# Loading the row of shift_k first and spreading it over the partitions during the warm-up

## The chip, the core and the metric

The kernel runs on one core of a Trainium2 chip. The core has TensorE (PE: matrix products; PEld: its weight loads), VectorE (DVE), ScalarE (ACT), GpSimd (POOL) and SyncE (SP), each with a queue of its own that it works through in order, and 16 DMA engines that all queues share. The metric is the time of one execution on the device, in microseconds (us); shown are the median of several runs and one execution recorded by the profiler.

## The reference

The reference is a forward pass of two branches and all of its gradients. S is 2048, D is 512, F is 1376, all tensors are bf16.

```python
xn = layernorm(q)                                  # no weights
k_shift = sum over t of k_pad[:, t:t+S] * shift_k[:, 3-t]     # four taps
kv = k_shift * v
y = causal_conv(kv, ssm_k) + kv * ssm_D            # by FFT over 2S
h = (xn @ w_gate) * (xn @ w_up)
out = q + xn * y + h @ w_down
# and the gradients of out with grad_out: q, k, v, shift_k, ssm_k, ssm_D, w_gate, w_up, w_down
```

shift_k has the shape (512, 4): four taps for each of the 512 channels. In the kernel the rows of the sequence lie over the 128 partitions and the channels along the free dimension, so each partition needs all 2048 numbers of shift_k. The tile skb (128 x 4 x 512) holds them, the same in each partition.

## The kernel before

The 2048 positions are held as 128 partitions times 16 rows, and worked on in eight chunks of two rows. A main strand (main, with ffn1 and yb inside) does the gated products of a chunk: up and gate into pgu (L512), the gradient through w_down into pdh (L518), products of them on VectorE (L532, L533), then output and input gradient (py, px). A side strand (side, with front and then groups) does the convolution: front forms k_shift and kv and takes all signals through the first half of the transform; groups does the spectral part. A pacing rule takes steps of the two strands in turn. Then follow the weight gradients and the rest.

Two kinds of order meet. From L656 to first.close() in tables(3), the order of the instructions on TensorE, VectorE and ScalarE is the order in which the program states them (a manual schedule). After that, the tile framework's planner orders each engine's instructions by its own estimate of when each is ready and by priorities (high_priority with SOON). So an instruction taken out can change the order of others.

**The front of the program, L643 to L669.** The transfers are issued first. load_x(0) loads the first two rows of q and grad_out on SyncE's queue (x_b, go_b); load_w on ScalarE's queue loads the first part of the weights w_down, w_up and w_gate (Wd, Wu, Wg); SyncE's queue goes on with the other weight parts, the second chunk, the row skr of shift_k (L650, one partition, 2048 numbers, 4 KB), the row of ssm_D, ssm_k (ssk, 2 MB) and further rows. A transfer has to wait for an earlier one, most often the eighth before it, because eight semaphores are used in turn. Then TensorE does 36 warm-up products of the identity with itself (warm, L658: transposes whose result nobody reads), VectorE forms small tables and the statistics of the first chunk (norm_stats, L664), TensorE transposes go_b (pe_t, L665) and the first part of Wd (wd_transposes, L666); ScalarE takes the square root (norm_std, L333) and copies both transposes out of PSUM (gt, WdT; the helper act, L235); VectorE normalizes the rows (norm_rows, L339 and L342) and copies their transpose (xt, L238). Another ten warm-up products follow (L669), then the products of ffn1 for chunk 0: pdh first, then pgu. ScalarE's Sin for the tables (L76) and its square root need different function tables, which an ACT_TABLE_LOAD instruction brings in.

**The spread of shift_k, L704 to L712.** It is the second half of late_loads, which front calls for b = 0, behind the four table steps. load_k issues the transfers of k (tile kh, L311 to L315). Then skr is spread: for each half of the 512 channels, two products of a column of ones (one partition, 128 wide; "rows" in the profile) with 128 channels x 4 taps of skr, 512 columns each, into a PSUM tile pskb of the pool P2 (three buffers). A copy brings each half from PSUM to skb and turns the order from channel-tap to tap-channel: half 0 on ScalarE (act, L235), half 1 on VectorE (dve, L238). skb is first read by pre(0) at L391, for ks_b, and in the backward pass at L1104.

Around it in the side strand: kernel_spec transposes ssk on TensorE (ptk, L415), VectorE copies that to SBUF (kn, L238), stage1 multiplies (pf, L370) and the result is copied to fst by ScalarE or, one of four, VectorE. norm(2), norm(3) and so on take statistics of the next rows (L326, L327).

Of the kernel before, what the change touches and what calls it, by code (L numbers as in the profile page):

```python
# [8 lines left out]
BF = mybir.dt.bfloat16  # L9
# [9 lines left out]
D = 512  # L19
F = 1376  # L20
R = 16
P = 128
# [168 lines left out]
def kernel(  # L191
# [24 lines left out]
    nc = tc.nc  # L216
# [17 lines left out]
    def act(o, i):  # L234
        nc.scalar.copy(o, i)  # L235
# [16 lines left out]
    def P2(name, shape, dt=F32):  # L252
        return ps2.tile(shape, dt, name=name, tag="p2")

    def P1(name, shape, dt=F32):
        return ps1.tile(shape, dt, name=name, tag="p1")

    ident = const.tile([P, P], BF, name="ident")
# [3 lines left out]
    skb = const.tile([P, 4, D], BF, name="skb")  # L262
# [11 lines left out]
    ones = rows[:, 1, 0:128]  # L274
# [6 lines left out]
    stp = st_es.enter_context(tc.tile_pool(name="stp", bufs=2, side="right"))  # L281
# [13 lines left out]
    def load_x(b):  # L295
        load_go(b, load_q(b))

    def load_q(b):
        x = stp.tile([P, 2, D], BF, name="x_b", bufs=4)
        nc.sync.dma_start(x[:], x_n[:, 2 * b:2 * b + 2, :])  # L300
        return x

    def load_go(b, x):
        go = stp.tile([P, 2, D], BF, name="go_b", bufs=3)
        nc.sync.dma_start(go[:], go_n[:, 2 * b:2 * b + 2, :])
        XG[b] = (x, go)

    def load_k():
        for i, t in enumerate(hds):
            z = t[96:97, NFB - 1].rearrange("p t s -> p (t s)")  # L310
            nc.sync.dma_start(ST["kh"][0:1, 0:3, :].rearrange("p r d -> p (r d)")[:, 768 * i:768 * i + 768], z)  # L311
        nc.sync.dma_start(ST["kh"][1:113, 0:3, :], k_n[0:112, R - 3:R, :])
        nc.sync.dma_start(ST["kh"][113:128, 0:3, :], k_n[112:127, R - 3:R, :])
        for r0 in range(0, R, R // 2):
            nc.sync.dma_start(ST["kh"][:, 3 + r0:3 + r0 + R // 2, :], k_n[:, r0:r0 + R // 2, :])  # L315

    def norm(b):
        norm_stats(b)
        norm_rows(b)
# [15 lines left out]
    def norm_rows(b):  # L335
        x, go = XG[b]
        rb = slice(2 * b, 2 * b + 2)
        xn = x
        nc.vector.reciprocal(rstd[:, rb], rstd[:, rb])  # L339
        for i in range(2):  # L340
            r = 2 * b + i
            nc.vector.tensor_scalar(xn[:, i, :], x[:, i, :], mv[:, r, 0:1], rstd[:, r:r + 1],  # L342
                                    op0=ALU.subtract, op1=ALU.mult)
        XG[b] = (xn, go)
        if b > 1:
            store_xn(b)
        NORMED.add(b)
# [4 lines left out]
    def load_v(b):  # L352
        v = stp.tile([P, 2, D], BF, name="v_b")
        nc.sync.dma_start(v[:], v_n[:, 2 * b:2 * b + 2, :])
        VB[b] = v
# [53 lines left out]
    def kernel_spec():  # L409
        def tr(r0):  # L410
            pt = P2("ptk", [P, 4, D], BF)
            for i in range(4):
                for c in range(NC4):
                    src = ssk[:, c, :].rearrange("d (p r) -> d r p", r=R)[:, r0 + i, :]
                    nc.tensor.transpose(pt[:, i, cs(c)], src, ident[:])  # L415
            kn = ST["st1"].tile([P, 4, D], BF, name="kn", tag="kn", bufs=KNB)
            with tc.high_priority(offset=SOON):
                dve(kn[:], pt[:])
            return kn
        kn = tr(0)  # L420
        yield
        for r0 in range(0, R, 4):
            for i in range(4):
                stage1(0, kn, i, r0 + i, dve if i == 2 else act)
                if i == 1 and r0 + 4 < R:
                    nx = tr(r0 + 4)
                yield
            kn = nx

    def wd_transposes(fa, fe):  # L430
        c0, c1 = 128 * fa, min(F, 128 * fe)
        m = 4 if fe - fa <= 4 else 2
        for ca in range(0, NC4, m):
            pw = P2("pw", [P, m, 16 // m * 128], BF)
            for c in range(ca, ca + m):
                for fb in range(fa, fe):
                    f0, fw = FBLK[fb]
                    nc.tensor.transpose(pw[:, c - ca, (fb - fa) * 128:(fb - fa) * 128 + fw], Wd[:fw, fb, cs(c)], ident[:fw, :fw])
            (act if ca or not fa else dve)(WdT[:, ca:ca + m, c0:c1], pw[:, :, :c1 - c0])
# [26 lines left out]
    def pe_t(src, name, eng):  # L466

        pt = P1("px8", [P, 2 * NC4, P], BF)
        for i in range(2):
            for c in range(NC4):  # L470
                nc.tensor.transpose(pt[:, NC4 * i + c, :], src[:, i, cs(c)], ident[:])
        t = xtp.tile([P, 2, NC4, P], BF, name=name)
        to = t[:].rearrange("p r c s -> p (r c) s")
        eng(to, pt[:])
        return t

    def warm(src, n):

        pt = P1("warm", [P, P], BF)
        for _ in range(n):  # L480
            nc.tensor.transpose(pt[:], src[:], ident[:])
# [15 lines left out]
    def ffn1(ch):  # L497
# [3 lines left out]
        for fb0 in range(0, NFB, 2):  # L501
# [21 lines left out]
            if ch == 0 and fb0 == 0:  # L523
                wd_transposes(*WPARTS[1])
            gu = gup.tile([P, 2, 2, 256], BF, name="gu")
# [3 lines left out]
            if ch == 0 and fb0 == 4:  # L529
                wd_transposes(*WPARTS[2])  # L530
            with tc.high_priority(offset=SOON):
# [101 lines left out]
    def load_w(eng, fa, fe):  # L633
        c0, c1 = 128 * fa, min(F, 128 * fe)
        full = (c1 - c0) // 128
        eng.dma_start(Wd[:, fa:fa + full, :], B_w_down[c0:c0 + 128 * full, :].rearrange("(fb p) d -> p fb d", p=128))
        if c0 + 128 * full < c1:
            eng.dma_start(Wd[:c1 - c0 - 128 * full, fa + full, :], B_w_down[c0 + 128 * full:c1, :])
        for W, src in ((Wu, B_w_up), (Wg, B_w_gate)):
            eng.dma_start(W[:, :, c0:c1], src[:, c0:c1].rearrange("(c p) f -> p c f", p=128))  # L640

    WPARTS = ((0, 2), (2, 6), (6, NFB))
    load_x(0)  # L643
    load_w(nc.scalar, *WPARTS[0])
    load_w(nc.sync, *WPARTS[1])
    x1 = load_q(1)
    load_w(nc.sync, *WPARTS[2])
    load_go(1, x1)
    skr = stp.tile([1, D, 4], BF, name="skr", tag="fst", bufs=4)
    nc.sync.dma_start(skr[:], A_shift_k.rearrange("(o d) j -> o d j", o=1))  # L650
    nc.sync.dma_start(Drow, A_ssm_D.rearrange("(o d) -> o d", o=1))
    nc.sync.dma_start(ssk[:], A_ssm_k.rearrange("(c p) s -> p c s", p=128))
    load_v(0)
# [1 line left out]
    load_v(1)  # L655
    first = ExitStack()  # L656
    first.enter_context(tc.manual_schedule(engines={nc.vector.engine, nc.scalar.engine, nc.tensor.engine}))
    warm(ident, 36)  # L658
    TB.forward_base()
    TB.inverse_base()  # L660
    TB.inverse_phases()
# [3 lines left out]
    gt0 = pe_t(XG[0][1], "gt", act)  # L665
    wd_transposes(*WPARTS[0])  # L666
    norm_rows(0)
# [33 lines left out]
            first.close()  # L701
            open_st1()

    def late_loads():  # L704
        load_k()

        for h in range(2):
            pb = P2("pskb", [P, 2, D])
            for q in range(2):
                d0 = 256 * h + 128 * q  # L710
                nc.tensor.matmul(pb[:, q, :], lhsT=ones, rhs=skr[:, d0:d0 + 128, :].rearrange("o d j -> o (d j)"), start=True, stop=True)
            (act, dve)[h](skb[:, :, 256 * h:256 * h + 256], pb[:].rearrange("p q (d j) -> p j (q d)", j=4))  # L712

    def front():
        for b in range(8):
            if b == 0:
                late_loads()
                with tc.issue_after(TB.last.ins):
                    norm(2)
            elif b < 6:  # L720
                norm(b + 2)
            if LATE:
                LATE.pop(0)()
            yield
            if b == 0:
                yield from kernel_spec()
                yield from wgu_transposes()
                WTS.append(True)
            if 0 < b < 7:
                load_v(b + 1)  # L730
            yield from pre(b)
            if b < 5:
                load_x(b + 3)
        LATE.pop(0)()
        yield
# [38 lines left out]
    pace = [170 / 71]  # L774
    gpool["es"] = ExitStack()
    side = seq(front(), groups())


# [448 lines left out]
```

## Time and profile before

| | |
|---|---|
| median of three runs | 480.31 us (479.93 to 480.77) |
| the profiled execution | 480.12 us |
| its span, first to last instruction | 478.3 us |
| busy in the span: PE, PEld | 469.2 us, 312.7 us |
| busy: DVE, ACT, POOL | 340.3 us, 305.6 us, 13.9 us |
| moved by DMA | 139.85 MB, mean 292 GB/s |
| first real product (pdh, L518) | starts at 9.17 us |
| the four products of pskb | from 25.75 us |
| first use of skb (ks_b, L391) | 36.30 us |

Times inside the profile count from the span's start. In a timeline row stand the start, the length (of the whole group, where several alike are merged), engine, line, operation, what is written and read, the count, and in brackets how long the engine was idle before it and what released it. In the page's slices a digit is the busy share of one fortieth of the span in tenths; 9 means 90% or more. A product counts as busy from its issue to its modelled end, so products in a row overlap.

### The profile page before, as it was taken

To read this page: it belongs to the slowest core of one execution; us is meant where nothing else is said; L and a number is where in the kernel's file an instruction comes from. 1 tells how busy PE (TensorE), PEld (TensorE's weight loads), DVE (VectorE), ACT (ScalarE), POOL (GpSimd) and SP (SyncE) were. 2 spreads that over 40 slices of the span, in tenths; PEclk is the share of its full clock that TensorE was granted. 3 is DMA by queue.
4 is the path that set the end of the run, shared out by engine and by line. 5 is a ranking of instruction groups with operands and counts; after the bars stand their busy time and mean duration, and the time that the engine had idled before them with its cause. 6 is when DMAs were issued, how large, how long until landed. Compare 5 with 4: busy or idle time off the path is not lost.

```text
span 478.3 us, 10403 instructions
## 1 busy us (share of the span) xinstructions
PE 469.2 (98%) x4293; PEld 312.7 (65%) x4293; DVE 340.3 (71%) x609; ACT 305.6 (64%) x349; POOL 13.9 (3%) x30
## 2 busy tenths in 40 slices
PE   8999999999999999999999999999999999999997
PEld 7876755547648547447447743566777787777785
DVE  6789989989366567686767877122257799599991
ACT  4957777759567778779779976275676545233241
POOL 8000000000000000000000000110000000000000
PEclk9999999999999999999999999999999999999999
DMA  8999899898998968967977469999999989999937
GB/s 273 375 378 365 295 299 312 314 322 313 313 295 291 265 199 267 279 205 246 293 240 240 153 236 357 348 330 318 328 383 379 372 264 321 319 270 281 286 134 238
DMA packets 111100, 139.85 MB, mean 292 GB/s; under 512 B 38827, under 2 KB 84304, under 8 KB 109518
## 3 DMA queue, kind: packets, MB, share of 16 engines
q1 hardware_dynamic: 109470, 137.85, 89.2%
q10 hardware_dynamic: 1584, 1.36, 1.0%
q8 instruction: 33, 0.54, 0.5%
q14 instruction: 13, 0.11, 0.1%
HBM read 67.08 MB, written 63.41 MB: 273 GB/s over the span
## 4 chain that ended last, share of the span: by engine, by line
PE 75%; DMA 12%; DVE 9%; SPq 1%; issue 1%; ACT 1%; ACTq 0%; DVEq 0%
PE px L555 14%; PE pgu L512 13%; PE pu L1050 11%; PE py L548 7%; PE pd L1014 6%; PE pdh L518 6%; PE pt L847 4%; PE pq L920 3%; PE ps L584 3%; PE pf L370 3%; PE pg L613 3%; DMA ssk<-in_A_ssm_k_dram 3%; DMA natT<-HDD 2%; DMA hb<-HDD 2%; DMA x_b<-in_A_q_dram 2%; DMA XN<-x_b 1%
## 5 line engine op out<-in xcount | busy, mean ns | idle before, releaser
L555 PE MATMUL px<-WT,hd 128*128 128x512 bf16 (+1 forms) x352 | 81.0, 380 | 0.0
L1050 PEld LDWEIGHTS <-xnC 128*128 128x128 bf16 x704 | 67.1, 98 | 8.3 <-issue 0.6
L555 PEld LDWEIGHTS <-hd 128*128 128x128 bf16 (+1 forms) x352 | 32.8, 98 | 44.4 <-issue 7.7
L235 ACT CAST gu<-pgu 128x1024 bf16<-128x1024 f32 (+1 forms) x48 | 45.4, 946 | 16.6 <-PE pgu L512 16.3
L235 ACT CAST GO<-pg 128x1024 bf16<-128x1024 f32 x48 | 46.3, 1016 | 13.7 <-issue 7.2
L235 ACT CAST SP<-ps 128x1024 bf16<-128x1024 f32 x47 | 45.6, 1027 | 13.7 <-PE ps L584 11.8
L600 DVE TENSOR_TENSOR T<-SP 128x2048 bf16<-128x2048 bf16 x24 | 29.4, 1223 | 34.8 <-ACT SP L235 34.7
L512 PE MATMUL pgu<-xt,Wu 128*128 128x256 bf16 (+1 forms) x352 | 53.1, 273 | 0.7 <-DVE kn L238 0.6
L512 PE MATMUL pgu<-xt,Wg 128*128 128x256 bf16 (+1 forms) x352 | 52.8, 273 | 0.0
L1050 PE MATMUL pu<-natd,xnC 128*128 128x256 bf16 x448 | 51.2, 273 | 0.0
L518 PE MATMUL pdh<-gt,WdT 128*128 128x256 bf16 (+1 forms) x352 | 46.9, 273 | 0.2 <-ACT WdT L235 0.2
L235 ACT CAST fst<-pf 128x1024 bf16<-128x1024 f32 x44 | 42.8, 1032 | 5.5 <-ACT fst L235 2.0
L512 PEld LDWEIGHTS <-Wu 128*128 128x128 bf16 (+1 forms) x352 | 33.0, 100 | 15.1 <-issue 10.2
L548 PE MATMUL py<-Wd,hd 128*128 128x512 bf16 (+1 forms) x176 | 41.4, 380 | 0.0
L235 ACT CAST og<-pu 128x1024 bf16<-128x1024 f32 (+1 forms) x11 | 10.9, 993 | 42.6 <-PE pu L1050 30.3
L518 PEld LDWEIGHTS <-WdT 128*128 128x128 bf16 (+1 forms) x352 | 34.9, 100 | 5.0 <-ACT WdT L235 0.4
L512 PEld LDWEIGHTS <-Wg 128*128 128x128 bf16 (+1 forms) x352 | 34.9, 100 | 3.6
L235 ACT COPY natd<-pt 128x2048 bf16<-128x2048 bf16 x14 | 26.2, 1875 | 12.2 <-PE pt L847 12.2
L533 DVE TENSOR_TENSOR hd<-gu,dh 128x1024 bf16<-128x1024 bf16 (+1 forms) x48 | 30.8, 642 | 0.8
L532 DVE TENSOR_TENSOR hd<-gu 128x512 bf16<-128x512 bf16 (+1 forms) x48 | 19.1, 398 | 16.0 <-ACT gu L235 16.0
L548 PEld LDWEIGHTS <-hd 128*128 128x128 bf16 (+1 forms) x176 | 16.5, 98 | 20.8 <-issue 3.1
L600 DVE TENSOR_TENSOR U<-SP 128x2048 bf16<-128x2048 bf16 x24 | 29.2, 1218 | 0.0
(177 smaller groups left out, 692.9 us busy)
## 6 DMA issues: line engine op xcount, KB each, us to landing
HDD<-hd SPq DMA_DIRECT2D x35, 384.0 KB, 4.6
FD<-fst SPq DMA_DIRECT2D x24, 512.0 KB, 4.9
X<-FD SPq DMA_DIRECT2D x24, 512.0 KB, 5.6
GD<-GO SPq DMA_DIRECT2D x24, 512.0 KB, 3.8
g<-GD SPq DMA_DIRECT2D x11, 1024.0 KB, 8.9
hb<-HDD SPq DMA_DIRECT2D x7, 1344.0 KB, 11.0
bb<-BX SPq DMA_DIRECT2D x8, 512.0 KB, 4.8
BX<-bx SPq DMA_DIRECT2D x7, 512.0 KB, 4.0
```

The lines of the kernel that those rows point to most:

```text
L235: nc.scalar.copy(o, i)
L370: nc.tensor.matmul(pf[:, c, :], lhsT=TB.W1[:, c, :], rhs=src[:, i, :], start=True, stop=not point)
L512: nc.tensor.matmul(pgu[:w, i, t, :], lhsT=W[:, c, f0:f0 + w], rhs=xt[:, :, c, :], start=(c == 0), stop=(c == NC4 - 1))
L518: nc.tensor.matmul(pdh[:w, i, :], lhsT=WdT[:, c, f0:f0 + w], rhs=gt[:, :, c, :], start=(c == 0), stop=(c == NC4 - 1))
L532: nc.vector.tensor_tensor(hd[:fw, fb0:fb0 + n, 0, :], gu[:fw, :n, 0, :], gu[:fw, :n, 1, :], op=ALU.mult)
L533: nc.vector.tensor_tensor(hd[:fw, fb0:fb0 + n, 1:3, :], gu[:fw, :n], dh[:fw, :n].unsqueeze(2).to_broadcast((fw, n, 2, 256)), op=ALU.mult)
L548: nc.tensor.matmul(py[:], lhsT=hd[:fw, fb, 0, ss], rhs=Wd[:fw, fb, :], start=(fb == 0), stop=(fb == NFB - 1))
L555: nc.tensor.matmul(px[:], lhsT=hd[:fw, fb, t, ss], rhs=W[:fw, fb, :], start=(t == 1 and fb == 0), stop=(t == 2 and fb == NFB - 1))
L600: tt(W[:].rearrange("p c a d -> p c (a d)"), A[:, i:i + 1].rearrange("p c a d -> p c (a d)").to_broadcast((P, 2, 2 * D)), B[:].rearrange(" ...
L847: nc.tensor.transpose(pt[:, r, :fw], hs[:, (r % 2) * 128:(r % 2) * 128 + 128], ident[:fw, :fw])
L1014: nc.tensor.matmul(pd[:fw, :], lhsT=nat_h(fb, r), rhs=goC[:, r, :], start=(r == 0), stop=(r == R - 1))
L1050: nc.tensor.matmul(pu[:, c, :, :fw], lhsT=xnC[:, r, cs(c)], rhs=nat_d(fb, r), start=(r == 0), stop=(r == R - 1))
```

## The change

The transfer of skr goes from its place on SyncE's queue to the head of ScalarE's queue, ahead of the first weights. The spread (the new function spread_k) is stated inside the warm-up: 14 warm-up products, the four products of the spread, ten more, 24 in place of 36. Both copies to skb are on ScalarE. Since all this lies in the manually scheduled front, the four products and the two copies stand where they are written: ahead of the transposes of go_b on TensorE, ahead of the square root on ScalarE. late_loads goes; front calls load_k alone.

```diff
+    def spread_k():
+        for h in range(2):
+            pb = P2("pskb", [P, 2, D])
+            for q in range(2):
+                d0 = 256 * h + 128 * q
+                nc.tensor.matmul(pb[:, q, :], lhsT=ones, rhs=skr[:, d0:d0 + 128, :].rearrange("o d j -> o (d j)"), start=True, stop=True)
+            act(skb[:, :, 256 * h:256 * h + 256], pb[:].rearrange("p q (d j) -> p j (q d)", j=4))
+
     WPARTS = ((0, 2), (2, 6), (6, NFB))
+    skr = stp.tile([1, D, 4], BF, name="skr", tag="fst", bufs=4)
+    nc.scalar.dma_start(skr[:], A_shift_k.rearrange("(o d) j -> o d j", o=1))
     load_x(0)
     load_w(nc.scalar, *WPARTS[0])
...
     load_go(1, x1)
-    skr = stp.tile([1, D, 4], BF, name="skr", tag="fst", bufs=4)
-    nc.sync.dma_start(skr[:], A_shift_k.rearrange("(o d) j -> o d j", o=1))
     nc.sync.dma_start(Drow, A_ssm_D.rearrange("(o d) -> o d", o=1))
...
-    warm(ident, 36)
+    warm(ident, 14)
+    spread_k()
+    warm(ident, 10)
...
-    def late_loads():
-        load_k()
-
-        for h in range(2):
-            pb = P2("pskb", [P, 2, D])
-            for q in range(2):
-                d0 = 256 * h + 128 * q
-                nc.tensor.matmul(pb[:, q, :], lhsT=ones, rhs=skr[:, d0:d0 + 128, :].rearrange("o d j -> o (d j)"), start=True, stop=True)
-            (act, dve)[h](skb[:, :, 256 * h:256 * h + 256], pb[:].rearrange("p q (d j) -> p j (q d)", j=4))
-
     def front():
         for b in range(8):
             if b == 0:
-                late_loads()
+                load_k()
```

## The prediction

> **What bounds the kernel now.** I read the page first: who is busy, and when.
>
> ```profile
> PE 469.2 (98%) x4293; PEld 312.7 (65%) x4293; DVE 340.3 (71%) x609; ACT 305.6 (64%) x349; POOL 13.9 (3%) x30
> ...
> PE   8999999999999999999999999999999999999997
> ...
> DVE  6789989989366567686767877122257799599991
> ACT  4957777759567778779779976275676545233241
> ```
>
> The span of 478.3 us is TensorE's: it is busy for 469.2 of it. So the sum is short: the end moves with the work that TensorE has once it runs, and with its idle time. That idle time, 9.1 us, lies mostly in the first 60 us. Second view, the timeline of the first 13 us:
>
> ```profile
> 4.80 0.69 DVE L326 BATCH_NORM_STATS2 stats<-x_b 128x6 f32<-128x512 bf16 x1 [0.81 <-DMA x_b<-in_A_q_dram]
> ...
> 6.11 1.03 PE L471 MATMUL px<-ident,go_b 128*128 128x128 bf16 x8 [0.65 <-DMA go_b<-in_grad_out_dram]
> ...
> 6.54 0.30 ACT L333 ACTIVATE rstd<-mv,eps_t 128x2 f32<-128x2 f32 x1 [2.97 <-DVE mv L327]
> ...
> 7.18 1.01 ACT L235 COPY gt<-px 128x1024 bf16<-128x1024 bf16 x1 [0.35 <-PE px L471]
> ...
> 8.09 1.02 ACT L235 COPY WdT<-pw 128x1024 bf16<-128x1024 bf16 x1
> ...
> 9.13 1.28 ACT L76 ACT_TABLE_LOAD   x1
> ```
>
> ScalarE's queue opens the gate: square root, copy of gt, copy of WdT, and the first real product (pdh, L518) starts at 9.17, right after that last copy. Nothing later makes up for a delay there: the table of stretches shows TensorE busy 4.00 of 4 us from 12 to 20, and none of its waits from 9.17 to 25 us is for a transfer. Third view, the timeline where the row of shift_k is spread today and what follows:
>
> ```profile
> 25.75 1.03 PE L711 MATMUL pskb<-skr,rows 1*128 1x512 bf16 x4
> ...
> 26.42 1.03 ACT L235 CAST skb<-pskb 128x1024 bf16<-128x1024 f32 x1
> ...
> 26.71 1.22 PE L415 MATMUL ptk<-ident,ssk 128*128 128x128 bf16 x16
> ...
> 27.79 1.22 DVE L238 CAST skb<-pskb 128x1024 bf16<-128x1024 f32 x1
> ...
> 28.93 1.22 DVE L238 COPY kn<-ptk 128x2048 bf16<-128x2048 bf16 x1
> ...
> 30.20 0.38 PE L370 MATMUL pf<-kn,W 128*128 128x512 bf16 x1 [0.20 <-DVE kn L238]
> ...
> 36.30 0.69 DVE L391 TENSOR_TENSOR ks_b<-kh,skb 128x1024 bf16<-128x1024 bf16 x1 [1.51 <-DMA kh<-in_A_k_dram]
> ...
> 44.37 0.59 PE L370 MATMUL pf<-kn,W 128*128 128x512 bf16 x2 [0.51 <-DVE kn L238]
> ```
>
> Here VectorE is the pacemaker. It is busy without a gap from 40 to 52 and nearly so to 60, and TensorE waits for it. Fourth view, stretches of 4 us (length, then busy time and count on PE, PEld, DVE, ACT, POOL, then clock, DMA share, GB/s):
>
> ```profile
> 40.00:44.00 4.00, 3.86 (x38) 3.04 (x36) 4.00 (x9) 2.25 (x4) 0.00 (x0) 1.00 1.02 379
> 44.00:48.00 4.00, 3.09 (x23) 2.23 (x23) 4.00 (x8) 2.89 (x5) 0.00 (x0) 1.00 1.07 299
> 48.00:52.00 4.00, 3.66 (x35) 2.71 (x33) 4.00 (x8) 3.26 (x4) 0.00 (x0) 1.00 1.06 298
> 52.00:56.00 4.00, 3.65 (x29) 2.83 (x29) 3.93 (x7) 1.83 (x4) 0.00 (x0) 1.00 1.03 379
> ```
>
> Over the eight stretches from 28 to 60 TensorE is idle for 2.0 of 32 us; the waits name kn and fst copies of VectorE for about 1.8 of that. From 64 to 128 it is busy 4.00 in nearly every stretch, so a lead or a lag at 60 us reaches the end.
>
> **The change, part by part.**
>
> *Taken out at 25.7 us.* Four products of 512 columns: the next work (ptk) starts at 26.71 instead of 25.74, so at most 0.97; by their spacing, (1.03 - 0.37)/3 = 0.22 each, 0.88. I take **-0.9**. ScalarE's copy (1.03) goes too, where ScalarE has room (busy 1.29 of the next 4 us): nothing. VectorE's copy (1.22) goes from the engine that sets the pace: below.
>
> *Put in at the front, TensorE.* 14 products in place of 36, at (4.02 - 0.31)/35 = 0.106 apart, end at 1.44 + 14 x 0.106 = 2.9. Then TensorE waits for skr, and its queue with it: ten warm-up products and the transposes of go_b. When does skr land? The trace has no transfer of one row at the start. Lower bound: the last ACT issue of the kernel, alone on the queues, is at 475.49, its first packet at 476.35, its last landing signal at 476.69; 1.2 us after 0.72 and some 0.45 to the waiting engine (x_b's last signal at 4.36, VectorE starts at 4.80) give 2.4, which means no wait. Upper bound: x_b, issued at the same moment, at 4.80. Between: the ACT queue's first packet today comes only at 2.66, 1.94 after its issue; plus 0.17 (first packet to last signal, as at 476) and 0.45 gives **3.3**. I take it, because it is the row of that very queue and moment. The clock is not open yet: the records show 313 ns for a 128-column warm-up product against 219 after the clock opens at 7.41. So a 512-column product needs 4 x 0.106 = 0.42: half one is in PSUM at 3.3 + 0.85 + 0.2 = 4.35, half two at 5.2. Ten products more end at 6.1, as go_b lands (6.11). TensorE itself is not late; the 12 warm-up products dropped stood in that wait.
>
> *Put in at the front, ScalarE.* The skr issue (0.35, as SP's for it at 11.54) goes ahead of three issues that end at 2.26: they end at 2.6. Wd, Wu and Wg of the first part start 0.35 later; the last lands near 9.3 and is used at 10.49, so that is covered. The order of the changed program, as built, has **two table loads** where there was one: one ahead of the skb copies, another ahead of the square root. First load to 3.95; copies, 1.03 each as at 26.42, from 4.4 to 6.46; second load, 1.28, to 7.75; square root at 7.75 instead of 6.54, 1.21 late. Its statistics are ready at 6.5, so nothing hides this except the 0.35 that ScalarE waits at 7.18 today. gt and WdT end 0.86 later, and pdh starts at 10.0: **+0.86**. VectorE's normalized rows come 1.2 late, xt at 10.3; the products that read it follow eight pdh (0.87) and start at 10.9: hidden. Bounds from the two landings: 2.9 or earlier gives +0.46 (then the matmuls and copies alone count), 4.8 gives 2.70 - 0.35 = +2.35.
>
> The Trainium skill (ScalarE: Activation LUTs, "What ACT_TABLE_LOAD costs") says that a switch of set takes 1283 ns plus some 1380 ns of drain. The load at 9.13 here starts 0.02 us after the copy before it ends, and the next activation starts at 10.42, 1.29 after the load's start: no drain shows. With that drain the front would cost 0.86 + 1.38 = 2.24 by the page, and the sum would be near rival 4's.
>
> *The queues.* skr leaves SP; each later transfer moves up one place, and most wait for the transfer eight places earlier. The DMA engines are saturated from 4 us on (share 1.0 to 1.1), so bytes and not issues decide. ssk, 2 MB, still lands near 25.1 and still holds back the stores and loads behind it; kh still lands near 36.3. Bounds: the wait of 0.5 us that one SP issue has there, either way.
>
> *The planner's new order.* VectorE loses 1.22 of copying ahead of kh and starts its front work about 0.9 late. As built, it now does one more bn_stats (0.67) and the two rows of norm 2 (0.73) ahead of the first ks_b. It ends ks_b near 37.0, against 37.64 today for ks_b and those rows, and has the bn_stats behind it: a lead of about 1.3 at the wait for kh, into which today's 1.5 us of idle time turn. TensorE's waits for VectorE (1.8) can shrink by the difference of the two leads, 1.3 against 0.04: at most 1.3, at least nothing, since kn copies are also moved behind other work. I take two thirds, because more of its stretch is unbroken than not: **-0.85**.
>
> Sum: -0.9 + 0.86 - 0.85 = **-0.9**. The profiled execution took 480.12 us (span 478.3 and 1.8 around it), so 479.2; the median shown, 480.31, is 0.19 above it: **479.4** as a median.
>
> **Rivals** (times as medians)**.**
> 1. *All of it comes back.* skr at 2.9, and 1.3 of TensorE's waits vanish: -0.9 + 0.46 - 1.3 = -1.7, 478.6. For it: the rows of 475 us, and the unbroken VectorE row. Against: the ACT queue's first packet at 2.66.
> 2. *The lead is not used.* The new order puts one of the kn copies behind more statistics, and TensorE waits as before: -0.9 + 0.86 = 0, 480.3. In effect the 1 us saved at 25.7 is paid back at 7.75.
> 3. *Slower: the row lands late.* skr shares engines with x_b and go_b and lands with x_b at 4.8. Copies from 5.9, second load to 9.24, square root 2.70 late, front +2.35; VectorE's lead is gone, nothing comes back: -0.9 + 2.35 = +1.45, 481.8. It decides from a landing at about 4.0 on: there the front costs 1.56, the lead gives back the rest of 0.7, and the sum is zero. For it: x_b's own first packets take 0.25 to 0.8 each. Against: skr is first in its ring and a single row.
> 4. *Slower: the switch between the copies and the square root costs more than one load.* I price it as one load's length again, 1.28, the nearest row: front 0.86 + 1.28 = 2.14, lead gone, -0.9 + 2.14 = +1.24, 481.5. Against it: nothing of the kind stands around the loads at 9.13 and 20.43. The Trainium skill's drain, named above, would do this.
>
> **Chances and numbers.** Forecast 0.40 (478.8 to 480.0), rival 1 0.22, rival 2 0.15, rival 3 0.17, rival 4 0.06. A measurement of this kernel can tell about 0.2%, 0.96 us, so the threshold of "faster" is 479.35, through the middle of my forecast. Faster: half of the forecast and nearly all of rival 1, 0.41. Same: the other half, nearly all of rival 2 and the edges of 1 and 3, 0.36. Slower: 3 and 4 but for their edges, and a little of 2, 0.23. The range, 478.2 to 481.5, leaves out about a tenth on either side: below, rival 1 with more than 1.3 given back; above, the far half of rivals 3 and 4. A clock that opens one stretch later, because TensorE pauses at 2.9, is inside it: eight pdh at half speed cost 0.87 at most.
>
> **What would show it.** In the profile after: skr's landing, as the start of the pskb products, at 3.3; two ACT_TABLE_LOAD of 1.28 ahead of the square root, and that at 7.75; the first pdh near 10.0; ptk right after pdh, about 0.1 earlier than 26.71; the wait for kh under 0.5 instead of 1.51; TensorE's idle time from 28 to 60 at 1.2 instead of 2.0. I am wrong if pskb starts after 4.0, if pdh starts after 10.6, or if kh lands over 0.5 away from 36.3.

## The result and the profile after

The changed kernel took 485.78 us (median of six runs, 484.48 to 488.52) against 480.72 us for the kernel before (479.93 to 481.20). The ratio is 1.010, with a 95% interval of 1.0076 to 1.0123: the change makes the kernel **slower by 1%**, some 5 us. (Ratios here and below leave out a few disturbed executions, medians do not.) The profiled execution took 485.05 us, its span is 483.3 us against 478.3 before.

The first view is the page of the kernel after: busy time by engine, and the row of the granted clock over 40 slices of 12.1 us.

```profile
PE 467.5 (97%) x4239; PEld 313.6 (65%) x4281; DVE 340.5 (70%) x608; ACT 307.8 (64%) x351; POOL 13.6 (3%) x30
...
PEclk9999999989999999999999999999999999999999
```

TensorE is busy for 1.7 us less than before (469.2), yet the span is 5.0 us longer: its idle time rose from 9.1 to 15.8 us. Not all of that is standing still: the weight loads fell by 12 (4293 to 4281), as the warm-up did, the recorded products by 54 (4293 to 4239), so some 42 records of products are missing and count as idle time. And the ninth slice of the clock row, around 97 to 109 us, shows an 8: the clock was not granted in full there. TensorE's lag at seven points places the loss, and it does not depend on those records: the lag is when a certain weight load starts (up to 259 us the n-th one of pgu, L512; behind it those of L1050), less when the same one starts in the profiled execution of before. "Clock opens" is when the trace's clock records go from half to full speed. The kernels below *after* are those of the experiments.

| kernel | clock opens | lag at 12.6 | 27.7 | 45.7 | 81.6 | 107.3 | 320.6 | 471.2 us |
|---|---|---|---|---|---|---|---|---|
| before | 7.41 | 0 | 0 | 0 | 0 | 0 | 0 | 0 |
| after | 13.47 | +3.02 | +1.91 | +0.67 | +0.49 | **+5.21** | +4.90 | +4.93 |
| e1_both | 7.92 | +1.11 | +1.13 | -0.27 | -0.34 | -0.43 | -0.23 | +0.20 |
| e1_again | 12.68 | +2.64 | +2.65 | +1.27 | +1.17 | +1.35 | +1.19 | +2.50 |
| e2_left_out | 6.09 | +0.54 | -0.58 | -1.23 | -1.07 | **+3.39** | +3.09 | +3.07 |
| e5_x3 | 12.69 | +2.64 | +1.53 | +0.30 | +0.11 | +1.32 | +1.11 | +3.36 |
| e6_ones | 11.08 | +1.33 | +1.33 | -0.03 | -0.12 | -0.21 | -0.51 | -0.18 |
| e7_both_sqrt | 9.73 | +0.71 | +0.71 | -0.47 | -0.47 | -0.06 | -0.36 | +2.60 |
| e8_x_two | 12.86 | +2.73 | +1.62 | +0.39 | +0.20 | +1.25 | +0.95 | +2.77 |
| e9_sqrt_x_two | 8.05 | +0.58 | -0.53 | -1.76 | -1.84 | -0.24 | +0.11 | +1.14 |
| e9_again | 8.00 | +1.00 | -0.11 | -1.34 | -1.53 | +0.09 | -0.13 | +1.66 |
| e10_xb | 8.68 | +1.52 | +0.41 | -0.82 | -1.01 | +0.31 | +0.39 | +3.99 |

The row of *after* tells the story. The front costs 3.0 us, nearly all of which is given back by 82 us. Then, between 85 and 107 us, some 60 us behind everything that the diff touches, 4.7 us are lost in one step, and they stay to the end.

**The front.** The timeline of the kernel after, from 3 us on:

```profile
3.05 1.88 PE L647 MATMUL pskb<-skr,rows 1*128 1x512 bf16 x4
...
4.12 1.93 ACT L235 CAST skb<-pskb 128x1024 bf16<-128x1024 f32 x2
...
6.06 1.28 ACT L333 ACT_TABLE_LOAD   x1
...
7.36 0.30 ACT L333 ACTIVATE rstd<-mv,eps_t 128x2 f32<-128x2 f32 x1
...
7.89 1.35 DVE L342 TENSOR_SCALAR x_b<-x_b,mv,rstd 128x512 bf16<-128x512 bf16 x2
...
8.81 1.09 PE L471 MATMUL px<-ident,x_b 128*128 128x128 bf16 x8 [0.99 <-DVE x_b L342]
...
9.70 1.27 PE L481 MATMUL warm<-ident,x_b 128*128 128x128 bf16 x10
...
11.03 1.86 PE L518 MATMUL pdh<-gt,WdT 128*128 128x256 bf16 x8
```

The row of shift_k is there by 3.05 (the products wait for nothing), the second table load stands between the copies and the square root, and the square root is 0.82 late. But pdh now waits for neither gt nor WdT: TensorE waits 0.99 for VectorE's normalized rows, then has ten warm-up products ahead of pdh, and all of them run at half speed: eight pdh span 1.86 instead of 1.05 us.

**The step at 98 us.** The same kernel's timeline; "SPq" is a DMA issue in SyncE's queue:

```profile
92.29 0.39 SPq L536 DMA_DIRECT2D HDD<-hd  x1
92.77 1.41 SPq L376 DMA_DIRECT2D FD<-fst  x1
...
94.11 0.68 DVE L550 TENSOR_TENSOR bx<-py,xb 128x512 bf16<-128x512 f32 x1
94.22 0.60 SPq L300 DMA_DIRECT2D x_b<-in_A_q_dram  x1
94.71 0.68 DVE L394 TENSOR_TENSOR ks_b<-ks_b,t_b 128x1024 bf16<-128x1024 bf16 x1
...
95.42 0.69 DVE L393 TENSOR_TENSOR t_b<-kh,skb 128x1024 bf16<-128x1024 bf16 x1
...
96.15 0.69 DVE L394 TENSOR_TENSOR ks_b<-ks_b,t_b 128x1024 bf16<-128x1024 bf16 x1
...
96.87 0.69 DVE L393 TENSOR_TENSOR t_b<-kh,skb 128x1024 bf16<-128x1024 bf16 x1
...
98.88 1.29 DVE L326 BATCH_NORM_STATS2 stats<-x_b 128x6 f32<-128x512 bf16 x2 [1.31 <-DMA x_b<-in_A_q_dram]
...
100.42 0.29 ACT L333 ACTIVATE rstd<-mv,eps_t 128x2 f32<-128x2 f32 x1 [6.16 <-DVE mv L327]
...
102.15 0.98 PE L370 MATMUL pf<-v_b,W 128*128 128x512 bf16 x2 [2.98 <-ACT fst L235]
```

And the kernel before at the same place:

```profile
90.38 0.60 SPq L300 DMA_DIRECT2D x_b<-in_A_q_dram  x1
...
94.24 0.68 DVE L550 TENSOR_TENSOR bx<-py,xb 128x512 bf16<-128x512 f32 x1
...
94.84 1.28 DVE L326 BATCH_NORM_STATS2 stats<-x_b 128x6 f32<-128x512 bf16 x2
...
96.90 0.29 ACT L333 ACTIVATE rstd<-mv,eps_t 128x2 f32<-128x2 f32 x1 [3.12 <-DVE mv L327]
```

The load of x_b for chunk 6 used to stand ahead of a store of hd (HDD, L536) in SyncE's queue, which is issued as soon as VectorE has written hd: its product L533 ends at 92.26, the store is issued at 92.29, and SyncE's longest wait there, 2.4 us, is for L533. Now it stands behind that store and a store of fst: issued 3.84 us later and landed 4.6 after that, at 98.8, where *before* could read it at 94.84. VectorE's order is new as well: in *before* the statistics follow the addition bx (L550) directly, in *after* four steps of the side strand (L394, L393) stand between and end at 97.56. Then the statistics wait another 1.31 us for x_b. So with x_b there in time they would still have started 2.7 us later than in *before*. The square root waits for the statistics, and ScalarE, which works in order, sits idle for 6.16 us with copies of PSUM tiles queued behind that square root. In *before* the same square root already held ScalarE for 3.12 us, and TensorE's buffered work just covered it. Twice as long is not covered: pf finds no free PSUM tile, and TensorE stands still for 2.98 us. Then the clock, the rate that TensorE is granted, closes, that is, falls to half. Stretches of the kernel after (length, then busy time and count on PE, PEld, DVE, ACT, POOL, then clock, DMA share, GB/s):

```profile
100.00:104.00 4.00, 1.63 (x4) 0.70 (x5) 3.60 (x10) 3.58 (x6) 0.00 (x0) 0.78 0.79 285
104.00:108.00 4.00, 4.00 (x16) 1.64 (x15) 2.84 (x8) 1.96 (x4) 0.00 (x0) 0.80 0.98 356
```

By the clock's own records it is at half speed from 102.21 to 105.63, 3.41 us. That costs 3.41 / 2 = 1.71, and with the 2.98 of standing still 4.69; the step between 85.1 and 107.3 us is 5.21 - 0.49 = 4.72. The step is accounted for, and with it nearly the whole loss of the profiled execution. The other five runs have the same mean granted clock, 0.996, or less, where *before*, run beside the experiments, has 0.999 or 1.000 in all runs but one. The Trainium skill (TensorE: Matmul & The Clock Gate, "Part 1: The HAM clock gate (the "warmup" mystery)") describes a free-running window of 3413 ns, and the half rate after an idle one; the trace agrees, with a closed stretch of 3.41 us behind one of 3.41 us in which TensorE stood still for 2.98.

### The profile page after: what moved, and what is told of

Read it like the earlier page. It is cut to its first block, busy times and chain, and to the rows that moved or that the text cites. A ratio compares the mean times of both kernels' runs of the same rounds, so it can differ in the third digit from the quotient of the medians.

```text
span 483.3 us, 10334 instructions
## 1 busy us (share of the span) xinstructions
PE 467.5 (97%) x4239; PEld 313.6 (65%) x4281; DVE 340.5 (70%) x608; ACT 307.8 (64%) x351; POOL 13.6 (3%) x30
## 2 busy tenths in 40 slices
DMA packets 111100, 139.85 MB, mean 289 GB/s; under 512 B 38827, under 2 KB 84304, under 8 KB 109518
## 4 chain that ended last, share of the span: by engine, by line
PE 68%; DVE 15%; DMA 9%; ACT 4%; issue 3%; SPq 1%; POOL 0%; ACTq 0%; DVEq 0%; POOLq 0%
PE px L555 14%; PE pgu L512 13%; PE pu L1050 8%; PE py L548 7%; PE pdh L518 6%; PE pd L1014 4%; PE ps L584 3%; DMA khC<-in_A_k_dram 3%; PE pg L613 3%; PE pf L370 2%; DMA natT<-HDD 2%; PE pq L920 2%; PE pt L847 2%; DMA kb<-KS 2%; DVE tk L1104 1%
## 5 line engine op out<-in xcount | busy, mean ns | idle before, releaser
L555 PE MATMUL px<-WT,hd 128*128 128x512 bf16 (+1 forms) x340 | 78.6, 379 | 1.6 <-issue 1.4
L1050 PEld LDWEIGHTS <-xnC 128*128 128x128 bf16 x704 | 67.1, 98 | 8.3 <-issue 0.6
L512 PE MATMUL pgu<-xt,Wu 128*128 128x256 bf16 (+1 forms) x352 | 53.5, 275 | 0.7 <-DVE kn L238 0.5
L512 PE MATMUL pgu<-xt,Wg 128*128 128x256 bf16 (+1 forms) x352 | 52.8, 273 | 0.0
L1050 PE MATMUL pu<-natd,xnC 128*128 128x256 bf16 x448 | 51.2, 273 | 0.0
L512 PEld LDWEIGHTS <-Wu 128*128 128x128 bf16 (+1 forms) x352 | 33.2, 101 | 14.9 <-issue 9.9
L512 PEld LDWEIGHTS <-Wg 128*128 128x128 bf16 (+1 forms) x352 | 35.0, 100 | 3.7
L533 DVE TENSOR_TENSOR hd<-gu,dh 128x1024 bf16<-128x1024 bf16 (+1 forms) x48 | 30.8, 642 | 0.8
## 6 DMA issues: line engine op xcount, KB each, us to landing
hb<-HDD SPq DMA_DIRECT2D x7, 1344.0 KB, 10.6
```

Of the source, the lines that this page charges most:

```text
L512: nc.tensor.matmul(pgu[:w, i, t, :], lhsT=W[:, c, f0:f0 + w], rhs=xt[:, :, c, :], start=(c == 0), stop=(c == NC4 - 1))
L533: nc.vector.tensor_tensor(hd[:fw, fb0:fb0 + n, 1:3, :], gu[:fw, :n], dh[:fw, :n].unsqueeze(2).to_broadcast((fw, n, 2, 256)), op=ALU.mult)
L555: nc.tensor.matmul(px[:], lhsT=hd[:fw, fb, t, ss], rhs=W[:fw, fb, :], start=(t == 1 and fb == 0), stop=(t == 2 and fb == NFB - 1))
L1050: nc.tensor.matmul(pu[:, c, :, :fw], lhsT=xnC[:, r, cs(c)], rhs=nat_d(fb, r), start=(r == 0), stop=(r == R - 1))
```

## The experiments

Two accounts were set against each other. **The order**: the planner's new order of the queues around 90 us makes the loss, whatever the front does. **The front**: the late pdh and the late opening of the clock make it, and the stall is only where they come out.

### e1_both: the new front, with the old spread kept

The changed kernel, with late_loads put back: skb is written twice, and the order behind the front is that of *before* but for four neighbouring transfers near 25 us (a store of HDD, two of XN, a load of x_b).

```diff
+    def late_loads():
+        load_k()
+        for h in range(2):
...
             if b == 0:
-                load_k()
+                late_loads()
```

> The front of the changed kernel (skr first, spread in the warm-up, both copies on ScalarE), and the late spread as well, which writes the same numbers to skb a second time. The planner's order of all later instructions is then that of the kernel before, but for one pair of transfers near 25 us. Theory A (order): the 5 us come from the stall of TensorE at 98 to 102 us, made by the new order of the transfers, in which x_b for chunk 6 stands two places later; the front alone costs little in the end. Then no stall near 98 us, clock not closed a second time, and the front's +0.5 at 82 us plus the 1.0 of products not removed: 480.7 + 1.5 = 482.2. Rival B (front): the delay of 3 us at the front is what makes the later stall, whatever the order: 485 to 486.

Measured: ratio 1.0044 (1.0020 to 1.0068), median 483.04 against 480.96. No stall at 98 us, and the lag stays between -0.2 and -0.5 from 46 to 320 us. So the order account holds for the step. The median is 0.8 above the 482.2 that it had named, and the profiled execution, 480.31, is the fastest of the ten; its clock opened at 7.92, in the changed kernel only at 13.47. That had to be looked at again.

### e1_again: the same kernel, a second profile

> The same kernel as the first experiment, for a second profile: there the clock opened at 7.9 us and the profiled execution took 480.3, but its timed runs had a median of 483.0. If the timed runs are those in which the clock opens late, this profile shows an opening at 10 to 13.5 us and a span 1.5 to 3 us longer, with TensorE's lag 2 to 3 us at 20 us. If the clock opens by 8 us again and the span is 480 or more all the same, the difference lies behind the front.

Measured: 482.63 us, clock opened at 12.68. The same program, with the same order, is 1.5 us later at 82 us (+1.17 against -0.34) and keeps that to 320 us. The moment at which the clock opens differs between executions of one kernel, and a late one is carried through here. If most of e1's timed executions open late, that is most of its 2.1 us over *before*; and its row lacks the gain of 1.11 from 12.6 to 27.7 us that the kernels without a late spread have.

### e2_left_out: the old front, without the spread

The kernel before, with the late spread taken out and skb filled with a constant, so that the outputs that depend on shift_k are not the right ones. From 20 us on, to 130 at least, the order of SyncE, ScalarE and VectorE is exactly that of the changed kernel.

```diff
+    nc.gpsimd.memset(skb[:], 0.01)
...
-        for h in range(2):
-            pb = P2("pskb", [P, 2, D])
...
```

> The kernel before with its old front; the late spread is left out altogether (skb is filled with a constant by GpSimd at the start, so the four products and two copies are missing). Its order of transfers and of ScalarE's instructions behind the front is exactly that of the changed kernel. Theory A (order): x_b for chunk 6 is issued near 93.5 instead of 90.4, ScalarE waits for its statistics with fst copies behind, TensorE stalls about 3 us near 97 to 101 and its clock may close: +4.65 of the stall less 1.0 for the products, 484. Rival B (front): with the old front nothing stalls, 480.7 - 1.0 or better, 479.5.

Measured: ratio 1.0057 (1.0029 to 1.0086), median 483.36. The timeline of e2 (its lines are numbered one higher):

```profile
91.29 0.52 SPq L377 DMA_DIRECT2D FD<-fst  x1
91.86 0.61 SPq L301 DMA_DIRECT2D x_b<-in_A_q_dram  x1
...
97.07 1.29 DVE L327 BATCH_NORM_STATS2 stats<-x_b 128x6 f32<-128x512 bf16 x2 [0.59 <-DMA x_b<-in_A_q_dram]
...
98.61 0.30 ACT L334 ACTIVATE rstd<-mv,eps_t 128x2 f32<-128x2 f32 x1 [5.91 <-DVE mv L328]
...
100.34 0.59 PE L371 MATMUL pf<-v_b,W 128*128 128x512 bf16 x2 [2.73 <-ACT fst L235]
```

A kernel that does *less* work, but for one memset on GpSimd, is slower. It leads by 1.07 us at 82 us, about what the four products were worth, and loses 4.46 in the same step: 2.73 of standing still, and 1.71 for a clock closed from 101.67 to 105.08. Its own front is only 0.54 late at 12.6 us, so the front account can't explain that; the order alone does. Here the statistics wait only 0.59 us for x_b: most of their delay is VectorE's order. In two of the six runs the clock did not close, and these were the shortest, 481.1 and 481.9.

### e5_x3 and e8_x_two: the changed kernel, with one load back in its place

Both are the changed kernel with one statement changed: the loads for chunk 6 (x_b, go_b) get a higher priority, in e5 by SOON (300), in e8 by 15. In e5 both go far ahead; in e8 x_b goes ahead of the two stores. The planner moves more with them: in e8 the load of xb falls behind that of go_b, and on VectorE the statistics of chunk 6 come ahead of bx and of the four steps that stood in front of them.

```diff
-            if b < 5:
+            if b == 3:
+                with tc.high_priority(offset=15):   # e5: SOON
+                    load_x(b + 3)
+            elif b < 5:
```

> The changed kernel with one edit: the loads of x_b and go_b for chunk 6 have a high priority in the planner, so that they are issued well ahead of 94 us. Theory A (order): the stall at 98 to 102 and the second closing of the clock are gone; what is left is the +0.5 that the trace shows at 82 us: 481.2, between 480.5 and 482. Rival B (front): 485 to 486, with TensorE idle near 98 all the same. Rival C: the early load takes the place of another that is then late, and a stall comes elsewhere: 483 or more with idle time of TensorE in another place.

> The changed kernel with the smallest edit that undoes the one reordering: the load of x_b for chunk 6 gets a slightly higher priority and stands ahead of the two stores (HDD and FD) behind which it stood; ScalarE's order stays the same up to 110 us. Theory A (order): x_b is issued near 90 instead of 94.2, its statistics come before ScalarE is through with its copies, TensorE's 3 us of idle time at 99 and the second closing of the clock go: 480.8 + 0.5 to 1.0 = 481.5, no step in TensorE's lag between 85 and 112 us. Rival B (the front's delay alone makes the stall): 485.5. Rival C (the lag of the earlier load shows up at another place, as the 0.8 us at 85.6 in the version with a high priority): 483.

Measured: e5 1.0042 (1.0016 to 1.0069), e8 1.0056 (1.0028 to 1.0085), where the changed kernel has 1.010. The timeline of e8:

```profile
88.78 0.73 SPq L300 DMA_DIRECT2D x_b<-in_A_q_dram  x1
...
91.91 0.39 SPq L536 DMA_DIRECT2D HDD<-hd  x1
...
93.74 1.28 DVE L326 BATCH_NORM_STATS2 stats<-x_b 128x6 f32<-128x512 bf16 x2
...
98.70 0.69 DVE L550 TENSOR_TENSOR bx<-py,xb 128x512 bf16<-128x512 f32 x1 [0.33 <-DMA xb<-in_A_q_dram]
...
99.45 0.59 PE L548 MATMUL py<-Wd,hd 128*128 128x512 bf16 x2 [0.99 <-DVE bx L550]
```

The 3 us stall is gone in both profiles, and the second closing of the clock in all nine runs of e5 and nine of ten of e8. So the place of this load, with what the planner moves along with it, is the cause of the step. Whether the load's place on SyncE or that of the statistics on VectorE weighs more is not shown: no run moves one without the other. And only about half of the 5 us came back; I had expected 481.5 of e8 and 481.2 of e5 and got 483.35 and 483.47, near the 483 that rival C named in both. Two things stand in the place of the stall. TensorE now waits 0.99 for an addition of VectorE (bx) at 99.45, in e5 0.80 for ScalarE (gu) at 86.4. And the profiles lose another 1.8 (e8) and 2.3 us (e5) behind 320 us, which the changed kernel's profile does not.

### e6_ones: one-partition products in the old warm-up

The kernel before, with products of one partition put where the changed kernel has its spread; nothing else moves.

```diff
-    warm(ident, 36)
+    warm(ident, 14)
+    pd1 = P2("pone", [P, 2, D])
+    for q in range(4):
+        nc.tensor.matmul(pd1[:, q % 2, :], lhsT=ones, rhs=ident[0:1, :].unsqueeze(1).to_broadcast((1, 4, P)), start=True, stop=True)
+    warm(ident, 10)
```

> The kernel before, with its late spread; only the first warm-up is changed: 14 products of the identity, four products of one partition and 512 columns (ones times a row of the identity, nobody reads them, no transfer to wait for), ten products of the identity, in place of 36. The order behind is that of the kernel before. Theory K (one-partition products do not open the clock): TensorE is as busy as before from 1.4 to 6, but the clock opens one activity window later, at 9 to 13.5 us instead of 7.4, and first pdh and pgu products take 1 us longer in all: 480.7 + 0.5 to 1.2. Rival P (phase, or the wait for the rows after 7.8 us): the clock opens near 7.4, and the time is 480.7.

Measured: ratio 1.0014 (0.9985 to 1.0042), so no difference that can be told. The timeline of e6:

```profile
3.05 1.88 PE L661 MATMUL pone<-ident,rows 1*128 1x512 bf16 x4
4.87 1.25 PE L481 MATMUL warm<-ident 128*128 128x128 bf16 x10
```

From 1.44 to 7 us TensorE hardly pauses, less than in *before*, which waits 0.65 for go_b. Yet the clock opens at 11.08 instead of 7.41, as theory K had it; the 0.5 to 1.2 us that it named do not show in the time. Products of one partition keep TensorE busy but do not seem to count for the clock: below. The 1.33 us that this costs at the front is gone at 46 us, because VectorE's wait for kh falls from 1.51 to 0.27.

### e7, e9, e10: towards a better version

e7 is e1 and e9 is e8, each with a square root of a constant ahead of the skb copies: the copies then need no table of their own, and the second load (1.28) goes. e10 is e9 with the loads of xb moved ahead as well. The cut shows the two lines that e5 and e8 do not have.

```diff
+    nc.scalar.activation(rstd[:, 0:1], eps_t[:, 0:1], ACTF.Sqrt)
...
-        nc.sync.dma_start(xb[:], x_n[:, 2 * ch:2 * ch + 2, :])
+        with tc.high_priority(offset=15):
+            nc.sync.dma_start(xb[:], x_n[:, 2 * ch:2 * ch + 2, :])
```

> The front of the changed kernel and the late spread as well (the order of the kernel before), with a square root of a constant ahead of the copies of skb, so that only one function table is loaded before the rows are normalized. Theory L (the second load is what makes the front late): the square root starts near 6.5 instead of 7.35, the transposes of x_b near 7.7 instead of 8.8, pdh near 9.3 to 9.5 instead of 10.3 to 11.0; the one idle gap of TensorE at 7.8 (1.0 us) goes, so the clock opens by 10.1 at the latest; 481.0, that is 2 us below the same kernel without the early square root. Rival D (the one-partition products keep the clock shut all the same, and that is the larger part): pdh earlier by 1, but the clock at 10 to 13, 482.5 or more.

> The changed kernel with both repairs: the early square root (one table load) and the load of x_b for chunk 6 ahead of two stores. Theory A with L: the front is late by under 1 us, which the wait for kh at 36 us absorbs; the four products and one copy of VectorE's are gone from 25.7 us, as in the run with the spread left out (a lead of 1.07 at 82 us); no stall: 480.9 - 0.9 = 480.0. Rival: the lead is lost again at another wait, 481 to 482; or the clock stays shut to 13 us, 481.

> As e9, but in the strand of output and input gradients the loads of the rows that are added (xb) are stated at a priority 15 places earlier too. In the built order one of them then stands a place earlier than KS in SP's queue around 90 us, and the VectorE addition that reads it (bx) stands ahead of the statistics of chunk 6 instead of behind the square root. Theory (e9's lead of 1.84 us at 82 us was lost to one wait of TensorE, 1.55 us at 98 us, for that addition): no idle time over 0.5 us of TensorE between 94 and 104 us, a lead of 1.3 to 1.9 us kept at 107 us, and a median of 479.6, 1.3 below the kernel before. Rival (the lead can't be kept, since the transfers of this stretch set the pace and another wait takes its place): a lead under 0.6 us at 107 us, and a median within 0.5 of that of e9 run beside it.

> The same kernel as e9, beside e10 on one chip, to tell a difference of a microsecond from the scatter between profiled executions. Theory: 480.5 to 481.5 as before, the clock opened between 6.5 and 10 us, a lead lost at 98 us. Rival (the moment of the opening differs from run to run and carries through): a profiled execution whose clock opens after 11 us is 1 to 1.5 us longer than one whose clock opens by 8.

Measured: e7 1.0036 (1.0010 to 1.0062), e9 1.0006 (0.9986 to 1.0025) and again 1.0008 (0.9985 to 1.0030), e10 0.9999 (0.9973 to 1.0025). The timeline of e9:

```profile
5.98 0.31 ACT L333 ACTIVATE rstd<-mv,eps_t 128x2 f32<-128x2 f32 x1
...
9.05 1.03 PE L518 MATMUL pdh<-gt,WdT 128*128 128x256 bf16 x8
...
97.96 0.59 PE L548 MATMUL py<-Wd,hd 128*128 128x512 bf16 x2 [1.55 <-DVE bx L550]
```

With one table load the square root is at 5.98, earlier than the 6.54 of *before*, pdh starts at 9.05, and e9 leads by 1.84 us at 82 us: the front of this change can be made to work. The lead is lost at 98 us, in one wait for bx. VectorE is busy without a gap from 92.67 to bx, at 97.22: the statistics and rows of chunk 6 now stand ahead of it. The 480.0 expected of e9 did not come (481.25, and 481.99 in e9_again, above its 480.5 to 481.5); the rival of a lead lost at another wait did. Both profiles opened their clock at 8.0, so e9_again's own rival, a late opening, was not met. e7 had the earlier square root and an opening at 9.73 as expected, but not the 481.0: its profile loses 3.0 us behind 320 us. e10 moves xb ahead, that wait goes, and another of the same stretch takes its place:

```profile
101.30 1.04 PE L370 MATMUL pf<-dy_b,W 128*128 128x512 bf16 x4 [1.16 <-DVE dy_b L383]
```

e10's lead of 1.01 at 82 us is a lag of 0.31 at 107. Its theory (lead kept, 479.6) fell, its rival (482.3 and 481.99 beside each other) held. No lead over 0.45 us at 82 us lasted to 107 us in any kernel (e2, e7, e9, e10); those of e1 and e6, under 0.35, did. Shifting one load there moved the wait on to the next. No version beat *before* by more than can be told.

## Why the prediction was wrong

The forecast was 479.4 us in a range of 478.2 to 481.5; it came out at 485.78, and none of the four rivals named the cause.

**The step that failed is "The queues".** It said that "bytes and not issues decide", and gave 0.5 us either way. The change takes one transfer, four products and two copies out of the planned part, and the planner reacted with another order, in which some 65 us later one load moved behind two stores on SyncE and the statistics that read it moved back by four steps on VectorE. Bytes were the same (139.85 MB in both profiles); the order cost 2.98 us of standing still and 1.71 of clock, where the prediction had allowed 0.5. e2 shows that this order is enough without the new front, e5 and e8 that the stall goes when that load, and with it the statistics, goes back. The prediction used the built order for ScalarE's front and for VectorE up to 60 us; the queues of SyncE, VectorE and ScalarE up to 110 us tell the rest. The row to look for was in the trace of before, the square root at 96.90 with 3.12 us idle ahead of it: a wait with little cover left.

**"Normalized rows 1.2 late ... hidden" failed.** TensorE's queue is in order, and the transposes of x_b and ten warm-up products stand ahead of pdh. The rows also took 1.35 instead of 0.86 us (560 and 870 ns each, against 412 and 534). So pdh came at 11.03, beyond the limit of 10.6 that the prediction set itself; with the clock open (e1) it comes at 10.29, and the front costs 1.11, not 0.86.

**"Nothing later makes up for a delay there" failed.** e1 and e6 lose 1.11 and 1.33 us at the front and have all of it back at 46 us, while VectorE's wait for kh shrinks from 1.51 to 0.31 and 0.27. Both keep the late copy on VectorE. So what *after* takes back between 27.7 and 81.6 us, 1.42, is not shown to come from the copy taken out, the prediction's -0.85. Of the kernels without that copy and without a lag at 27.7 us, e2 gains 0.49 there and e9 1.31; what separates those two was not tried.

**The clock was mis-sized**: "0.87 at most". It opened 6.06 us later. Against e1, whose front is the same and whose clock opened at 7.92, that is 3.02 - 1.11 = 1.91 us at the front. e1_again, opened at 12.68, shows 2.64 - 1.11 = 1.53 there and 1.51 still at 82 us.

**Right** were two table loads, and no drain behind the second: 6.06 + 1.28 = 7.34, square root at 7.36. So rival 4's dearer switch does not show. The drain of 1380 ns that the Trainium skill (ScalarE: Activation LUTs, "What ACT_TABLE_LOAD costs") adds does not show here.

The row was there earlier than the forecast of 3.3. (That sum took 0.17 from the first packet to the last signal, where its own figures, 476.35 and 476.69, are 0.34 apart.) The products start at 3.05 without a wait, as e6's do, which read no transfer. That is the prediction's lower bound (2.9 or earlier, front +0.46), and the square root came where that bound puts it, 0.82 late. That the front was dearer all the same lies in pdh's place behind the rows and in the clock.

The four products were worth 3.02 - 1.91 = 1.11 (forecast 0.9). The wait for kh vanished, as the row of the kernel after shows, with no idle time in brackets:

```profile
37.73 0.69 DVE L391 TENSOR_TENSOR ks_b<-kh,skb 128x1024 bf16<-128x1024 bf16 x1
```

But VectorE had no lead there: this ks_b ends at 38.42, not near the 37.0 of the forecast. TensorE's idle time from 28 to 60 us fell from 2.00 to 1.53, not to 1.2. Taken together, the lag at 82 us is +0.49; less the 1.91 of the late clock that would be about -1.4, against a forecast of -0.9. That is an estimate, no run shows it, and it does not confirm the sum, whose terms came out otherwise. But even this lead would not have lasted: the assumption that "a lead or a lag at 60 us reaches the end", because TensorE is busy nearly throughout, fails for leads. e9 leads by 1.84 at 82 us and by 0.24 at 107. A busy TensorE at today's pace does not show that the queues behind it could keep up with a faster one.

**Open** is the last stage. Behind 320 us the profiles differ by 0 to +3.6 us, even among runs of one kernel (e9: +0.61 and +2.30 at 421 us), with waits for loads of HDD (natT, L1014; hb) and for VectorE's kd. Whether e5 and e8 are slower there because of their order or by chance was not tried; in the changed kernel's own profile nothing is lost there. Why the rows of L342 took longer isn't settled either, but it goes with what GpSimd does at that time. In *after*, e1, e1_again, e5 and e8 they start at 7.9, beside GpSimd's L167 and L172, and take 859 to 875 and 557 to 560 ns. In e2 they start at 7.91 as well, but GpSimd is then at L153, L154 and L157, and they take 411 and 406. No run changes GpSimd's work alone.

## What to carry to other kernels

Where a planner orders the queues, an instruction taken out in one place can move a load behind a store in another: compare the built order on every queue, SyncE's, VectorE's and ScalarE's first, over the whole span, and look at each move of a load past an issue that waits for data, and of the instructions that read it. In the profile of before, find the waits that are barely covered (an in-order engine idle for 3 us with PSUM copies behind it); they are where a small shift turns into a stall. And a lead at one point is worth only what the queues of the next stretch can follow.

## What the runs showed of the hardware

*Products of one partition and the clock.* The clock changes at the ends of windows of 3.41 us, whose phase differs from run to run: the stretches at full speed are whole numbers of them (88.75 us in *after* is 26 times 3.413, 95.57 in e2 is 28 times, 471.04 in *before* and e1 138 times), and the closed ones last 3.41. For windows ahead of the opening, the share of time in products that use all 128 partitions (full), in one-partition products, and idle:

| window (us) | full | one partition | idle | clock |
|---|---|---|---|---|
| before 4.00 to 7.41 | 0.81 | 0 | 0.19 | opens |
| e2 2.68 to 6.09 | 0.84 | 0 | 0.16 | opens |
| e1 4.51 to 7.92 | 0.87 | 0.10 | 0.03 | opens |
| e6 4.25 to 7.66 | 0.81 | 0.18 | 0.01 | stays |
| after 3.23 to 6.64 | 0.52 | 0.48 | 0 | stays |
| after 6.64 to 10.05 | 0.71 | 0 | 0.29 | stays |
| e7 2.91 to 6.32 | 0.49 | 0.51 | 0 | stays |

A window of *after* and one of e7, full with products to the last, left the clock closed, and about half of them was one-partition products; windows with 0.81 to 0.87 of full-height products and up to 0.19 idle opened it. So a one-partition product counts for less than a full-height one: by *after*, with a limit at 0.81, at most (0.81 - 0.52) / 0.48 = 0.6 as much, an estimate. If it counts for nothing, e6 fits as well, and the limit lies near 0.81 of full-height ones; but e6 stayed shut and *before* opened at the same 0.81, a difference that modelled ends of products can't settle. Transposes count: the windows of e2 and *before* hold nothing else. The Trainium skill (TensorE: Matmul & The Clock Gate, "Part 4: PE-mode transpose") says that they do not count as busy time in the same way; these runs show no sign of that.

*The spread of single executions.* The moment at which the clock opens puts 1.5 us between two executions of one program at 82 us (e1 and e1_again): a single profile of such a kernel can't judge a change of 1 us.
